# Attention scores as 64x64 matmuls on the four quarters of the tensor array, and the product with v in one group

## The chip, the cores and the metric

The kernel runs on one core of one Trainium2 chip. Its time is the device time of one execution in microseconds (us); the figure for a kernel is the median of its runs. TensorE is written PE in the profile, its weight loads PEld, VectorE DVE, ScalarE ACT, GpSimd POOL, and SP is the engine whose queue issues nearly all transfers.

## What is computed

A sliding-window attention (4 sequences of 576 tokens, 8 heads of 64, each token sees itself and the 63 tokens before it), then a gated product, then a soft mixture of experts.

```python
scores = scale * np.matmul(q, k.transpose(0, 1, 3, 2))
mask = (rel >= 0) & (rel < 64)                      # rel = query position - key position
attn = softmax(np.where(mask, scores, -1e9))
x = np.matmul(attn, v)                              # [4, 8, 576, 64] -> x [2304, 512]
x = ((x @ w_a) * (x @ w_b)) @ w_out                 # w_a, w_b [512, 1536], w_out [1536, 512]
logits = x @ phi                                    # 8 experts x 4 slots
slots = softmax(logits, axis=0).T @ x               # through each expert: relu(slots @ w1) @ w2
out = softmax(logits, axis=1) @ expert_outputs      # [2304, 512]
```

## The kernel before, in words

The 2304 tokens are 18 tiles of 128. A tile has two blocks of 64 tokens (`b` = 0, 1). A block's window is the 128 keys of the block before it and of itself. The 8 heads are four pairs (`u` = 0 to 3); the two heads of a pair (`h` = 0, 1) lie in the two halves of the partitions, 64 rows each.

**Scores** (`att_q`, `att_k`, `att_s`). `att_q` and `att_k` transpose q and k of a tile, so that a head's 64 features lie on partitions. `att_s` makes for each block and pair the scores [2 heads x 64 queries, 128 keys] in a PSUM bank for each block, `s0` and `s1`. The first six tiles (`t < NPLAIN`) do this with two matmuls of 64 rows and 64 columns each (line 279): head 0 on the array's upper left quarter, head 1 on its lower right one. The twelve tiles from 6 on do it with one matmul of the full 128x128 array (line 283); for these, `att_q` writes q between zeros (`att_z` clears the place once), so that the other head's features add nothing. A 32-bit matmul shows in the trace as two records. Then DVE adds the mask and takes the row maximum (line 294), ACT takes the exponential (line 301), `att_n` divides, `att_pt` transposes the probabilities (`tp`), and `att_pv` multiplies them with v (line 342) into the bank `xps`: 8 matmuls of 128 rows and 64 columns for block 0 as soon as its probabilities are transposed, and 8 for block 1 one slot of the schedule later. The two heads write the two column halves in turn.

**The rest.** `glu` is the gated product: for a tile 3 blocks of 512 columns for w_a and for w_b, each 12 matmuls (`psa`, `psb`, line 449). The `r_` functions turn its result (`tg`), make logits (`lps`, line 485, 32 columns of the array for each of four matmuls side by side) and keep running sums (`ups`). Last come the experts, whose weights (`xw`) are fetched into places that the attention and the gated product leave.

**What sets the order.** The start is written out by hand in the text `STARTUP`, for all five engines: `As0` is the next piece of `att_s` of tile 0, `Av0.1` that of `att_pv` of tile 0, block 1; `Sa2.0` issues the load of a piece of w_a, `Da2.0` decodes it, `Po3` is a piece of the work on w_out. It covers attention of tiles 0 to 4 and the decoding of the gated product's weights. From there on only PE's order is fixed, by the numbered slots of `at(...)`; a scheduler orders the other engines. A tile's scores stand at slot `s`, its products with v at `s + 3` and `s + 4`, and its gated product begins at `s + 6` or later. SP issues transfers in the order of its queue; the two places for v (`lda` for the window of block 0, `ldb` for that of block 1) are single, so that the next tile's v waits until `att_pv` has read this tile's.

Of the kernel before, what the change touches and what calls it, by code (L numbers as in the profile page):

```python
# [20 lines left out]
P = 128  # L21
STOP = 0
STARTUP = """
    Ak0 Tq0 Aq0 Tq0 Sb0.0 Aq0 Sa0.2 Db0.0 Ak0 Sb0.2 Db0.0 Ak0 As0 Da0.2 As0 Da0.2 Tq1 Db0.0 Db0.2 Db0.0
    Tq1 Sa0.0 Sa0.1 Aq1 As0 As0 Tq2 Db0.0 As0 Db0.0 Ak1 Da0.2 Db0.0 An0.0 An0.0 Ak1 Aq1 Ak1 As0 Da0.2
    Db0.2 Db0.2 As1 Db0.2 Da0.0 Db0.2 An0.1 As1 Ak2 Da0.2 Da0.0 An0.0 As1 Da0.0 Tq2 Db0.2 Da0.2 Da0.1
    Sb0.1 Aq2 As1 Da0.2 An0.1 Ap0.0 Da0.0 Da0.0 Sb0.3 Aq2 Tv0 Db0.1 Ak2 An0.1 Ap0.0 Da0.1 Db0.2 Ap0.1
    Db0.3 Da0.0 An1.0 An1.0 Ak2 Db0.1 Db0.1 Da0.1 As1 Tv0 Av0.0 Ap0.1 Av0.1 As1 Db0.1 Tq3 As2 Da0.1
    Av0.1 Db0.1 As2 Da0.1 An1.1 An1.1 Db0.1 Ak3 Av0.1 Db0.3 Sa0.3 Da0.1 As2 Da0.0 An1.0 Aq3 Da0.3 Tq3
    Sa1.0 Gb0.0 Sa1.1 Da0.3 Ap1.0 An1.1 Da0.3 Tv1 Tv1 Aq3 Da0.1 Ga0.0 Db0.3 As2 Da0.3 Ap1.0 Ak3 Db0.3  # L30
    Ga0.0 Tq4 Ak3 Sb1.0 Ga0.0 Db0.1 Da0.3 Ap1.1 Da1.0 Da1.1 As3 An2.0 As2 Db0.3 Da1.1 Da1.1 As3 Da0.3
    Db0.3 Gb0.0 Da1.0 Av1.0 Ap1.1 Sa1.2 Av1.1 Sa1.3 Da0.3 As2 Da1.0 Av1.1 Gb0.0 Da1.1 An2.0 Db0.3 Da1.0
    An2.1 Da1.0 Ga0.0 Ga0.0 An2.1 Gb0.0 Da1.1 An2.0 Av1.1 Gb0.0 Tq4 Ap2.0 As3 Db1.0 Da1.0 Ga1.0 Aq4
    Gb1.0 Ak4 Po1 Da1.2 Db1.0 Ga1.0 Ga1.0 Da1.0 Ap2.0 Gb1.0 Db1.0 Da1.1 Tv2 Da1.3 Gb1.0 Da1.2 Ak4 As3
    Sb1.1 Tv2 Db1.0 Da1.1 Aq4 Da1.2 An2.1 Ak4 Ga1.0 Sb1.2 Da1.3 Da1.2 Db1.0 Da1.3 Sb1.3 Ga1.0 Da1.2 As3
    Gb1.0 Da1.2 Da1.3 Ap2.1 Po1 An3.0 Po1 Da1.2 Da1.3 Db1.0 Ga0.1 Db1.0 Po1 Ap2.1 As4 Ga0.1 Po4 Po1
    Ga0.1 As4 Po1 Gb1.0 Da1.3 Av2.0 Db1.1 As3 As4 Da1.3 Db1.2 Po1 An3.0 Db1.1 Db1.1 An3.0 Db1.2 Ga0.1
    Tv3 Ga0.1 Db1.1 Po1 Po3 Db1.3 Db1.2 Po1 Db1.1 Db1.1 Ph0 Db1.3 Db1.2 Av2.1 Gb0.1 Sa2.0 Sa2.1 Ga1.1
    Av2.1 Po4 Ga1.1 Db1.2 Po4 Av2.1 An3.1 Po4 Db1.3 Ga1.1 An3.1 Db1.3 Ga1.1 Db1.1 Ga1.1 Ap3.0 Db1.2 Tv3
    Gb0.1 Ga2.0 Ga2.0 Ga2.0 As4 Db1.2 Po3 Ga2.0 As4 Da2.0 Ga2.0 Po1 An3.1 Db1.3 Po3 Sa2.2 Po4 Ap3.1  # L40
    An4.0 Db1.3 As4 Db1.3 Da2.0 Gb0.1 Ga2.1 Po3 An4.0 Po7 Po4 Po3 Ga2.1 Po3 Po4 Ga2.1 Po3 Gb0.1 Gb0.1
    Ap3.0 Po4 Av3.0 Ga2.1 Da2.1 Da2.1 Ap3.1 Da2.1 Av3.1 Gb2.0 Po3 Gb2.0 Da2.0 Po1 Tv4 Av3.1 Da2.1 Sa2.3
    Gb2.0 Gb2.0 Ri0 Tq5 Po1 Sb2.1 Ga2.1 Av3.1 Da2.0 Ga3.0 Da2.1 Da2.0 Po0 Ga3.0 Da2.2 Gb2.0 Da2.0 Da2.2
    An4.0 Po4 Po3 Gb1.1 Po1 Da2.0 Da2.2 Sb2.0 Gb1.1 Tv4 Da2.1 Gb1.1 Ga3.0 Po5 Da2.3 Da2.2 Po7 Ga3.0
    Da2.2 Po7 Da2.3 Gb1.1 Po7 Da2.2 Po4 An4.1 Tq5 Da2.1 Da2.2 Ga3.0 Po7 Da2.3 An4.1 Ga0.2 Gb1.1 Po0
    Da2.3 Po7 Ap4.0 Ga0.2 Ga0.2 Gb2.1 Po4 Ga0.2 Da2.3 Db2.0 Da2.3 Po4 Sb2.2 Db2.0 Po7 Da2.3 Po0 Ap4.0
    Po5 Ga0.2 Gb2.1 An4.1 Po4 Gb2.1 Gb2.1 Ga0.2 Ga0.2 Db2.0 Po0 Ga0.2 Po3 Po7 Po0 Av4.0 Db2.0 Po0 Ga0.2
    Po6 Ga1.2 Po5 Db2.0 Po5 Ga1.2 Ga1.2 Po3 Ga1.2 Po3 Po5 Po7 Po5 Ga1.2 Po0 Db2.2 Gb2.1 Ga1.2 Po2 Db2.0
    Po5 Db2.2 Po0 Po5 Po3 Ga1.2 Db2.1 Db2.1 Db2.2 Po7 Po7 Gb3.0 Ga1.2 Db2.0 Ga1.2 Db2.1 Gb3.0 Po2 Po7
    Db2.2 Gb3.0 Po0 Db2.1 Ga3.1 Db2.2 Po5 Gb3.0 Po6 Ga3.1 Sb2.3 Po7 Po2 Gb3.0 Po5 Po5 Ga3.1 Db2.1 Po2  # L50
    Po6 Db2.2 Db2.1 Po2 Po2 Po6 Ga3.1 Ap4.1 Ga3.1 Db2.2 Po6 Po6 Po2 Db2.3 Gb3.1 Ga2.2 Ga2.2 Po5 Gb3.1
    Gb3.1 Po5 Po8 Po0 Db2.1 Ak5 Gb3.1 Ga2.2 Db2.3 Po9 Db2.3 Po0 Db2.3 Po0 Ak5 Ga2.2 Ga2.2 Po6 Po0 Gb3.1
    Ap4.1 Po8 Ga2.2 Po2 Gb0.2 Ak5 Gb0.2 Ga2.2 Db2.3 Av4.1 Po8 Po8 Po8 Po2 Gb0.2 Po2 Ga2.2 Po8 Db2.3
    Gb0.2 Po11 Db2.3 Gb0.2 Po2 Gb0.2 Po6 Tv5 Po2 Gb0.2 Po10 Gb0.2 Ga2.2 Tv5 Po2 Po8 Ga3.2 Po9 Gb0.2 Po6
    Ga3.2 Ga3.2 Po6 Po11 Gb1.2 Gb1.2 Po6 Ga3.2 Po9 Po8 Gb1.2 Gb1.2 Ga3.2 Gb1.2 Ga3.2 Po6 Po11 Po9 Po8
    Po10 Po10 Gb1.2 Po9 Po6 Gb1.2 Ga3.2 Po8 Gb1.2 Rt0.0 Po9 Po8 Gb1.2 Ga3.2 Po9 Po9 Gb3.2 Rt0.0 Aq5 Po9
    Po8 Po11 Po10 Av4.1 Po11 Po8 Po11 Gb3.2 Gb3.2 Gb3.2 Aq5 Po11 Gb3.2 Po10 Po9 Ga3.2 Po11 Po9 Po10 Po10
    Gb3.2 Po11 Po10 Po9 Rt0.2 Gb3.2 Po9 Po10 Gb3.2 Rt0.2 Rt0.1 Gb3.2 Rt1.0 Po10 Po10 Gb2.2 Gb2.2 Po10
    Gb2.2 Gb2.2 Gb2.2 Po10 Po11 Gb2.2 Gb2.2 Po11 Gb2.2 Gb2.2 Rt1.0 Po11 Rt0.1 Av4.1 Po11
# [955 lines left out]
```

## Time and profile before

| | us |
|---|---|
| median of 3 runs | 579.15 (578.6 to 579.62) |
| the profiled execution, by its span (no other time of it is listed) | 577.4 |
| PE busy | 540.5 (94%) |
| DVE busy | 297.6 (52%) |
| ACT busy | 229.8 (40%) |
| POOL busy | 76.5 (13%) |

The span runs from the first to the last instruction. The median lies 1.75 us above it, for what lies around the span and for the spread of the runs. Matmuls overlap, so PE's busy time says that PE had work, not that it worked at its peak.

### The profile page before, as it was taken

What the parts mean: (1) busy time and instruction counts of PE and PEld (TensorE: products, weight loads), DVE (VectorE), ACT (ScalarE), POOL (GpSimd) and SP (SyncE); (2) the same over time, 40 slices, a digit from 0 to 9 for tenths busy, and PEclk for the clock granted to TensorE, in tenths of its full rate; (3) what the DMA queues carried; (4) which work ended last, traced back from release to release, by engine and by line L of the source; (5) the groups of instructions that cost most, each with busy time, mean ns of one, the idle gap of its engine ahead of it and who ended that gap; (6) DMA issues with size and microseconds to landing.
All of it is one profiled execution on the core that took longest, in us unless ns stands there. A gap on an engine that the chain in (4) does not pass through costs nothing.

```text
span 577.4 us, 11537 instructions
## 1 busy us (share of the span) xinstructions
PE 540.5 (94%) x4531; PEld 429.9 (74%) x4531; DVE 297.6 (52%) x861; ACT 229.8 (40%) x675; POOL 76.5 (13%) x110
## 2 busy tenths in 40 slices
PE   4588899999999999999999999999999999989993
PEld 3476667889887879787888888888888767953442
DVE  3999999974444444353634443454555311142222
ACT  5767664544524343443523333433454211133013
POOL 4555465331000000000000000000000000020000
PEclk9789899999999999999999999999999999999997
DMA  9975747495030302020212203022212499889997
GB/s 267 266 224 182 242 137 212 145 257 183 0 75 1 75 18 58 18 57 19 56 27 48 56 19 74 17 59 56 56 38 74 152 351 339 317 289 346 341 357 245
DMA packets 110822, 83.00 MB, mean 144 GB/s; under 512 B 77616, under 2 KB 98608, under 8 KB 110768
## 3 DMA queue, kind: packets, MB, share of 16 engines
q1 hardware_dynamic: 109808, 79.12, 46.2%
q0 software_dynamic: 960, 3.15, 1.4%
q8 instruction: 36, 0.59, 0.4%
q14 instruction: 18, 0.15, 0.1%
HBM read 74.38 MB, written 7.86 MB: 142 GB/s over the span
## 4 chain that ended last, share of the span: by engine, by line
PE 77%; DVE 13%; DMA 4%; issue 2%; ACT 1%; SPq 1%; POOL 0%; POOLq 0%; ACTq 0%
PE psb L449 24%; PE psa L449 23%; PE tg L142 5%; PE s L283 4%; PE xps L342 3%; PE lps L485 3%; PE tp L142 2%; PE ups L560 2%; PE h L883 2%; DVE w L374 2%; DVE w L378 2%; PE ops L917 2%; DMA st<-in_moe_w_a_dram 2%; DVE w L368 1%; PE tq L142 1%
## 5 line engine op out<-in xcount | busy, mean ns | idle before, releaser
L449 PE MATMUL psa<-wha,x 128*128 128x512 f32 (+1 forms) x576 | 160.4, 347 | 2.1 <-DVE x L352 1.2
L449 PE MATMUL psb<-whb,x 128*128 128x512 f32 (+1 forms) x576 | 161.3, 348 | 1.1 <-DVE g L459 1.1
L449 PEld LDWEIGHTS psa<-wha,x 128*128 128x128 f32 x576 | 101.4, 189 | 18.3 <-DVE x L352 2.0
L449 PEld LDWEIGHTS psb<-whb,x 128*128 128x128 f32 x576 | 101.3, 190 | 14.7 <-issue 2.4
L449 PE MATMUL psa<-wla,x 128*128 128x512 f32 (+1 forms) x288 | 97.3, 338 | 1.2 <-POOL wla L424 1.2
L449 PE MATMUL psb<-wlb,x 128*128 128x512 f32 (+1 forms) x288 | 97.2, 337 | 0.0
L459 DVE TENSOR_TENSOR g<-psb,asb 128x512 f32<-128x512 f32 (+1 forms) x57 | 37.7, 661 | 89.2 <-PE psb L449 75.0
L455 ACT COPY asb<-psa 128x512 f32<-128x512 f32 (+1 forms) x57 | 32.1, 563 | 103.8 <-PE psa L449 103.4
L301 ACT ACTIVATE pr<-pr,nmx 128x128 f32<-128x128 f32 x144 | 55.9, 391 | 36.7 <-DVE nmx L294 36.7
L449 PEld LDWEIGHTS psa<-wla,x 128*128 128x128 f32 x288 | 54.7, 190 | 6.9 <-POOL wla L424 2.1
L449 PEld LDWEIGHTS psb<-wlb,x 128*128 128x128 f32 x288 | 54.8, 190 | 4.6 <-POOL wlb L424 0.2
L471 ACT COPY gT<-tg 128x512 f32<-128x512 f32 x54 | 31.4, 584 | 37.1 <-PE tg L142 37.0
L252 POOL COPY kTs<-kTs 128x256 f32<-128x256 f32 x17 | 8.2, 480 | 270.8 <-DVE kTs L263 266.1
L142 PE MATMUL tg<-ident,g 128*128 128x128 f32 x216 | 33.9, 280 | 0.7 <-DVE g L459 0.4
L331 DVE COPY pT<-tp 128x512 f32<-128x512 f32 x13 | 9.0, 691 | 47.9 <-PE tp L142 47.9
L294 DVE CUSTOM_DVE_ANT_0 pr<-s,masks 128x128 f32<-128x128 f32 x144 | 32.6, 285 | 1.8 <-PE s L283 1.0
L142 PEld LDWEIGHTS tg<-ident,g 128*128 128x128 f32 x216 | 24.7, 146 | 10.5 <-issue 7.3
L301 ACT ACTIVATION_READ_ACCUMULATOR pr<-pr,nmx 128x1 f32 x144 | 27.2, 189 | 0.0
L329 ACT COPY pT<-tp 128x512 f32<-128x512 f32 x23 | 13.4, 583 | 29.7 <-PE tp L142 29.7
L142 PE MATMUL tp<-ident,pr 128*128 128x128 f32 x144 | 22.9, 282 | 1.1 <-POOL pr L319 1.1
L283 PE MATMUL s<-kTs,qTs 128*128 128x128 f32 x192 | 23.5, 275 | 0.0
L350 ACT CAST x<-xps 128x512 fp32r<-128x512 f32 x18 | 10.5, 584 | 30.8 <-PE xps L342 30.8
(138 smaller groups left out, 754.3 us busy)
## 6 DMA issues: line engine op xcount, KB each, us to landing
xw<-in_moe_w_dram SPq DMA_DIRECT2D x39, 512.0 KB, 6.8
xw<-in_moe_w_dram SPq DMA_DIRECT2D x50, 256.0 KB, 5.9
st<-in_moe_w_b_dram SPq DMA_DIRECT2D x12, 512.0 KB, 5.3
st<-in_moe_w_a_dram SPq DMA_DIRECT2D x12, 512.0 KB, 5.9
st<-in_moe_w_out_dram SPq DMA_DIRECT2D x12, 512.0 KB, 4.7
out_dram<-ob SPq DMA_DIRECT2D x18, 256.0 KB, 3.9
ldq<-in_q_dram SPq DMA_DIRECT2D x16, 256.0 KB, 3.6
ldk<-in_k_dram SPq DMA_DIRECT2D x16, 256.0 KB, 3.4
```

The costliest lines, as they stand in the source:

```text
L142: nc.tensor.transpose(o, i, ident)
L283: nc.tensor.matmul(sp[:, u], lhsT=qT[:, 2 * u + b].rearrange("p h w -> p (h w)"), rhs=kTs[:, t % 2, u, W * b:W * b + P],)
L294: nc.vector.tensor_tensor_reduce(out=pr[:, u], in0=sps[b][:, u], in1=mk, scale=1.0, scalar=HUGE, op0=ALU.add, op1=ALU.min, accum_out=nmx[: ...
L301: nc.scalar.activation(out=pr[:, u], in_=pr[:, u], func=ACTF.Exp, scale=-1.0, bias=nmx[:, i:i + 1], accum_out=sm[:, i:i + 1],)
L329: nc.scalar.copy(out=pT, in_=tp)
L342: nc.tensor.matmul(xps[W * h:W * h + W, u, W * b:W * b + W], lhsT=vt[:, 2 * u + h, :], rhs=st["pT", b][:, u, W * h:W * h + W],)
L374: nc.vector.scalar_tensor_tensor(out=i, in0=hi, scalar=-(1 << 30), in1=i, op0=ALU.bitwise_and, op1=ALU.bitwise_or)
L449: nc.tensor.matmul(ps[:, cols], lhsT=l[:, kk], rhs=r, start=(n == 0), stop=(n == 3 * KD - 1))
L455: nc.scalar.copy(out=asb[:, cols], in_=ps[:, cols])
L459: nc.vector.tensor_tensor(out=gts[t][:, gcols], in0=ps[:, cols], in1=pas.pop((t, fg))[:, cols], op=ALU.mult)
L471: nc.scalar.copy(out=gT, in_=tp)
L485: nc.tensor.matmul(lps[32 * i:32 * i + 32], lhsT=wphi[:, 4 * fg + i], rhs=gT[:, i], start=(n == 0), stop=(n == len(fgs) - 1),)
```

## The change

- All 18 tiles take their scores from 64x64 matmuls, four for each pair: rows by head, columns by block. Head `h` has the PSUM bank `s{h}`, and block `b` the partition half; before, a bank was a block's and a partition half a head's. For the first six tiles this replaces the two-quarter form, for the other twelve the full one.
- `att_s` is cut after pairs 1 and 3, where it was cut after block 0 and block 1. Each half now writes both banks.
- The mask is stored as four blocks of 64 keys, two of which are picked for a tile, and DVE reads and writes the 128 keys of a row as two runs of 64.
- `att_q` is one ACT copy for every tile, into two buffers in turn; DVE's half of the copy and `att_z` are gone.
- `att_pv` is one group of 16 matmuls at the place where block 1's 8 stood. The transposed probabilities (`pT`) get a third buffer, since both are held until then.

```diff
-            nc.gpsimd.affine_select(
-                out=m, in_=m, pattern=[[0, 2], [1, P]], compare_op=ALU.is_gt,
...
+        qT = qTs[:, t % 2]
+        nc.scalar.activation(out=qT, in_=tq, func=ACTF.Copy, scale=-SCALE)
         sts[t] = {"qT": qT}
-        for h in range(2):
-            r = slice(W * h, W * h + W)
-            src = tq[r].rearrange("p u (b w) -> p (u b) w", b=2)
-            if h:
-                nc.vector.tensor_scalar(out=qT[r, :, h], in0=src, scalar1=-SCALE, scalar2=None, op0=ALU.mult)
-            else:
-                nc.scalar.activation(out=qT[r, :, h], in_=src, func=ACTF.Copy, scale=-SCALE)
...
-        for b in range(2):
-            sp = ps_s.tile([P, 4, P], F32, tag=f"s{b}", name=f"s{b}")
-            sps.append(sp)
-            for u in range(4):
-                if t < NPLAIN:
-                    for h in range(2):
-                        r = slice(W * h, W * h + W)
-                        nc.tensor.matmul(
-                            sp[r, u], lhsT=qT[r, u, W * b:W * b + W], rhs=kTs[r, t % 2, u, W * b:W * b + P],
-                        )
-                    continue
-                nc.tensor.matmul(
-                    sp[:, u], lhsT=qT[:, 2 * u + b].rearrange("p h w -> p (h w)"),
-                    rhs=kTs[:, t % 2, u, W * b:W * b + P],
-                )
-            yield
+        sps = [ps_s.tile([P, 4, P], F32, tag=f"s{h}", name=f"s{h}") for h in range(2)]
+        for u in range(4):
+            for h in range(2):
+                r = slice(W * h, W * h + W)
+                for b in range(2):
+                    c = slice(W * b, W * b + W)
+                    nc.tensor.matmul(
+                        sps[h][c, u], lhsT=qT[r, u, c], rhs=kTs[r, t % 2, u, W * b:W * b + P],
+                    )
+            if u % 2:
+                yield
...
-    def att_pv(t, b):
+    def att_pv(t):
...
+        for b in range(2):
+            vt = loaded[t]["b" if b else "a"]
+            c = slice(W * b, W * b + W)
+            for u in range(4):
+                for h in range(2):
+                    nc.tensor.matmul(
+                        xps[W * h:W * h + W, u, c], lhsT=vt[:, 2 * u + h, :], rhs=st["pT", h][:, u, c],
+                    )
...
-        at(s + 3, att_pv, t, 0)
         at(s + 3, att_pt, t, 1)
-        at(s + 4, att_pv, t, 1)
-        if t == NPLAIN:
-            at(s - 3, att_z)
+        at(s + 4, att_pv, t)
...
-    Db0.3 Da0.0 An1.0 An1.0 Ak2 Db0.1 Db0.1 Da0.1 As1 Tv0 Av0.0 Ap0.1 Av0.1 As1 Db0.1 Tq3 As2 Da0.1
+    Db0.1 Db0.1 Da0.1 As1 Tv0 Ap0.1 Av0 As1 Db0.1 Tq3 As2 Da0.1 Av0 Db0.1 As2 Da0.1 An1.1 An1.1 Db0.1 Ak3 Av0
```

The order of the instructions shows it at three places. On PE, the scores of tile 7 stand between the gated product (`psb`) and the logits (`lps`), before:

```order
L449 MATMUL psb<-wlb_1321,x 128x256
L449 MATMUL psb<-whb_1320,x 128x256
L283 MATMUL s_2384<-kTs,qTs 128x128 x4
L283 MATMUL s_2389<-kTs,qTs 128x128 x4
L485 MATMUL lps<-gT,wphi 32x128 x12
L449 MATMUL psa<-wha_324,x 128x512
```

and in the changed kernel (the last four of eight such rows, two matmuls each, for the two blocks):

```order
L259 MATMUL s_2390<-kTs,qTs 64x128 x2
L259 MATMUL s_2391<-kTs,qTs 64x128 x2
L259 MATMUL s_2390<-kTs,qTs 64x128 x2
L259 MATMUL s_2391<-kTs,qTs 64x128 x2
L460 MATMUL lps<-gT,wphi 32x128 x12
L424 MATMUL psa<-wha_325,x 128x512
```

Eight matmuls of the whole array have become sixteen of a quarter, at the same place. On PE again, the product with v of a later tile, block 0 (`lda`), before:

```order
L449 MATMUL psa<-wla_674,x 128x512
L449 MATMUL psa<-wha_673,x 128x512
L342 MATMUL xps<-pT,lda 64x64 x8
L142 MATMUL tp<-ident,pr 128x128 x4
L560 MATMUL ups<-g,dt 32x384 x4
```

and in the changed kernel, where that place has no `xps` any more and the 8 matmuls stand a slot later, ahead of block 1's:

```order
L424 MATMUL psb<-wlb_838,x 128x512
L424 MATMUL psb<-whb_837,x 128x512
L320 MATMUL xps<-pT,lda 64x64 x8
L320 MATMUL xps<-pT,ldb 64x64 x8
L139 MATMUL tq<-ident,ldq 128x128 x4
```

In the start, on PE, the scores of tile 4 (`s_702`, `s_720`) and the product with v of tile 2, before:

```order
L279 MATMUL s_720<-kTs,qTs 64x128 x8
L342 MATMUL xps<-pT,lda 64x64 x8
L449 MATMUL psa<-wha_673,x 128x512
L449 MATMUL psa<-wla_674,x 128x512
L449 MATMUL psa<-wha_673,x 128x512
L142 MATMUL two<-ident,wo 128x128 x4
L342 MATMUL xps<-pT,ldb 64x64 x8
```

and in the changed kernel:

```order
L259 MATMUL s_703<-kTs,qTs 64x128 x2
L259 MATMUL s_704<-kTs,qTs 64x128 x2
L424 MATMUL psa<-wha_674,x 128x512
L424 MATMUL psa<-wla_675,x 128x512
L424 MATMUL psa<-wha_674,x 128x512
L139 MATMUL two<-ident,wo 128x128 x4
L320 MATMUL xps<-pT,lda 64x64 x8
L320 MATMUL xps<-pT,ldb 64x64 x8
```

The reading of `lda` has moved behind three matmuls of the gated product and four transposes. SP's queue and the other engines keep their order, but for the operations that are gone or new and three swaps of neighbours.

## Rows read from the trace of the kernel before

**Rows 1.** Windows: length; busy PE, PEld, DVE, ACT, POOL; clock, DMA share, GB/s.
```profile
14.00:112.00 98.00, 82.51 (x628) 63.94 (x629) 96.93 (x208) 61.12 (x165) 51.60 (x49) 0.93 0.71 205
112.00:455.00 343.00, 342.10 (x2930) 288.75 (x2929) 163.97 (x542) 135.45 (x430) 14.38 (x23) 1.00 0.23 58
455.00:577.00 122.00, 109.45 (x928) 71.79 (x926) 31.55 (x92) 25.80 (x66) 4.75 (x15) 0.98 0.94 324
```

**Rows 2.** PE's timeline, full-array scores of two tiles: start, length, line, operation, records.
```profile
200.44 1.95 PE L283 MATMUL s<-kTs,qTs 128*128 128x128 f32 x16
202.31 0.86 PE L485 MATMUL lps<-gT,wphi 128*32 128x128 f32 x24
...
227.86 1.95 PE L283 MATMUL s<-kTs,qTs 128*128 128x128 f32 x16
229.64 0.27 PE L142 MATMUL dps<-ident,e 128*128 128x128 f32 x1
```

**Rows 3.** PE's timeline, two-quarter scores of tiles 4 and 5, and their neighbours.
```profile
57.70 0.40 PE L449 MATMUL psa<-wha,x 128*128 128x512 f32 x1
58.02 1.09 PE L279 MATMUL s<-kTs,qTs 64*64 64x128 f32 x16
59.05 0.69 PE L342 MATMUL xps<-pT,lda 128*64 128x64 f32 x16
...
145.00 1.96 PE L279 MATMUL s<-kTs,qTs 64*64 64x128 f32 x32
```

**Rows 4.** PE's timeline around a product with v, and transposes behind a gated product.
```profile
209.58 0.60 PE L142 MATMUL tp<-ident,pr 128*128 128x128 f32 x4
...
212.87 0.39 PE L449 MATMUL psa<-wla,x 128*128 128x512 f32 x1
213.09 0.39 PE L449 MATMUL psa<-wha,x 128*128 128x512 f32 x1
213.41 0.69 PE L342 MATMUL xps<-pT,lda 128*64 128x64 f32 x16
214.03 0.66 PE L142 MATMUL tp<-ident,pr 128*128 128x128 f32 x4
```

**Rows 5.** Tiles s, lps, xps: one record's ns (min/median/max), first and last start.
```profile
L279 PE MATMUL s<-kTs,qTs x192: 269/269/473, 8.5 to 146.7; 64*64 64x128 f32 x192
...
L485 PE MATMUL lps<-gT,wphi x432: 272/273/298, 146.9 to 511.3; 128*32 128x128 f32 x144
...
L342 PE MATMUL xps<-pT,lda x288: 222/222/366, 24.6 to 449.5; 128*64 128x64 f32 x144
```

**Rows 6.** Tiles qTs, kTs and tp: copies on ACT, DVE and POOL.
```profile
L243 DVE TENSOR_SCALAR qTs<-tq x12: 694/695/697, 165.9 to 426.6; 64x512 f32<-64x512 f32 x12
L234 ACT ACTIVATE qTs<-tq x6: 577/588/632, 5.2 to 135.4; 128x512 f32<-128x512 f32 x6
L223 POOL MEMSET qTs<- x1: 952/952/952, 147.1 to 147.1; 128x1024 f32 x1
...
L263 DVE COPY kTs<-tk x13: 678/691/692, 119.7 to 430.4; 128x512 f32<-128x512 f32 x13
...
L331 DVE COPY pT<-tp x13: 690/691/692, 159.3 to 450.4; 128x512 f32<-128x512 f32 x13
```

**Rows 7.** Timelines of SP and ACT, and pieces of the chain that ended last.
```profile
59.77 0.38 SPq L207 DMA_DIRECT2D lda<-in_v_dram  x1
...
61.36 0.95 SPq L408 DMA_DIRECT2D st<-in_moe_w_a_dram  x2
65.05 0.37 SPq L207 DMA_DIRECT2D ldb<-in_v_dram  x1
...
61.36 4.23 DMA st<-in_moe_w_a_dram
...
72.90 0.65 ACT L366 ACTIVATE w<-st 128x512 f32<-128x512 f32 x1
...
111.21 0.43 PE pp L591 x8
```

More of the change, by code (lines that the diff above doesn't have):

```diff
@@ L125, in swa_glu_softmoe_kernel @@
     ri = const.tile([P, P], F32, name="ri")
-    masks = const.tile([P, 2, P], F32, name="masks")
+    masks = const.tile([P, 4, W], F32, name="masks")
     sel = const.tile([P, 2, 4, NS], F32, name="sel")
@@ L153, in build_ident @@
             nc.gpsimd.affine_select(
-                out=m, in_=m, pattern=[[0, 2], [1, P]], compare_op=ALU.is_gt,
+                out=m[:, 3], in_=m[:, 3], pattern=[[-1, W]], compare_op=ALU.is_ge,
+                fill=BIG, base=0, channel_multiplier=1,
+            )
+            nc.gpsimd.affine_select(
+                out=m[:, 0:3], in_=m[:, 0:3], pattern=[[0, 3], [1, W]], compare_op=ALU.is_gt,
                 fill=BIG, base=0, channel_multiplier=-1,
             )
-            nc.gpsimd.affine_select(
-                out=m, in_=m, pattern=[[0, 2], [-1, P]], compare_op=ALU.is_ge,
-                fill=BIG, base=W, channel_multiplier=1,
-            )
-        nc.gpsimd.memset(masks[:, 1, 0:W], BIG)
+            nc.gpsimd.memset(m[:, 1 - h], BIG)
     def build_ri():
@@ L215, in swa_glu_softmoe_kernel @@
     xts = {}
-    qTs = att.tile([P, 2 * 4 * P], F32, name="qTs", bufs=1)
+    qTs = att.tile([P, 2, 4, P], F32, name="qTs", bufs=1)
     kTs = att.tile([P, 2, 4, W + P], F32, name="kTs", bufs=1)
-    NPLAIN = NFIRST + 2
-    def att_z():
-        nc.gpsimd.memset(qTs, 0.0)
     def att_q(t):
@@ L299, in att_s @@
             for u in range(4):
-                i = 4 * b + u
+                i = 4 * h + u
                 nc.scalar.activation(
@@ L305, in att_s, with att_n @@
             yield
-    def att_n(t, b):
+    def att_n(t, hh):
         st = sts[t]
-        h = slice(4 * b, 4 * b + 4)
+        h = slice(4 * hh, 4 * hh + 4)
         rs = small.tile([P, 4, 1], F32, tag="rs", name="rs")
@@ L324, in att_pt @@
         for u in range(4):
-            transpose(tp[:, u], st["pr"][b][:, u])
+            transpose(tp[:, u], st["pr"][hh][:, u])
         yield
-        pT = att.tile([P, 4, P], F32, tag="pT", name="pT")
-        if b == 0 or t <= NFIRST:
+        pT = att.tile([P, 4, P], F32, tag="pT", name="pT", bufs=3)
+        if hh == 0 or t <= NFIRST:
             nc.scalar.copy(out=pT, in_=tp)
@@ L331, in att_pt @@
             nc.vector.tensor_copy(pT, tp)
-        st["pT", b] = pT
-    def att_pv(t, b):
+        st["pT", hh] = pT
+    def att_pv(t):
         st = sts[t]
-        if b == 0:
-            st["x"] = ps_t.tile([P, 4, P], F32, tag="x", name="xps", bufs=1)
-        xps = st["x"]
-        vt = loaded[t]["b" if b else "a"]
-        for u in range(4):
-            for h in range(2):
-                nc.tensor.matmul(
-                    xps[W * h:W * h + W, u, W * b:W * b + W],
-                    lhsT=vt[:, 2 * u + h, :],
-                    rhs=st["pT", b][:, u, W * h:W * h + W],
-                )
-        if b == 1:
-            yield
-            x = xp.tile([P, 2, 4, P], F32R, tag="x", name="x")
-            nc.scalar.copy(out=x[:, 0], in_=xps)
-            yield
-            nc.vector.tensor_tensor(out=x[:, 1], in0=xps, in1=x[:, 0].bitcast(F32), op=ALU.subtract)
-            xts[t] = (x[:, 0], x[:, 1])
-            del sts[t], loaded[t]
+        xps = ps_t.tile([P, 4, P], F32, tag="x", name="xps", bufs=1)
+        for b in range(2):
+            vt = loaded[t]["b" if b else "a"]
+            c = slice(W * b, W * b + W)
+            for u in range(4):
+                for h in range(2):
+                    nc.tensor.matmul(
+                        xps[W * h:W * h + W, u, c], lhsT=vt[:, 2 * u + h, :], rhs=st["pT", h][:, u, c],
+                    )
+        yield
+        x = xp.tile([P, 2, 4, P], F32R, tag="x", name="x")
+        nc.scalar.copy(out=x[:, 0], in_=xps)
+        yield
+        nc.vector.tensor_tensor(out=x[:, 1], in0=xps, in1=x[:, 0].bitcast(F32), op=ALU.subtract)
+        xts[t] = (x[:, 0], x[:, 1])
+        del sts[t], loaded[t]
     whi, wlo = {}, {}
@@ L585, in project_phi @@
         yield
-        wT = att.tile([P, 4, P], F32, tag="pT", name="wT")
+        wT = att.tile([P, 4, P], F32, tag="pT", name="wT", bufs=3)
         nc.scalar.copy(out=wT, in_=tp)
```

88 lines of the change are left out of this document (39 added, 49 removed).

## Prediction

> **What bounds the kernel now.** I read the windows of the trace first, cut where the stages change [rows 1]. From 14 to 112 us DVE is busy for 96.93 of 98 us: the start, in which the weights are decoded, is DVE's. From 112 to 455 us PE is busy for 342.10 of 343 us at the full clock, DVE for 164 and ACT for 135: here a microsecond less on PE is a microsecond less in all, as long as PE finds no new wait. All work of the attention for tiles 5 to 17 lies in this stretch. After 455 us the DMA engines are busy to 94%: the experts' weights go into places that the attention and the gated product have left. Nothing is changed there; it starts when the attention ends, so I take it to move as a whole.
>
> Then the timelines of PE. A tile's scores on the full array are 16 records in 1.95 us; the last lasts 0.27 us, so they start 0.112 us apart. From the first to the next work it is 1.78 us where full-array work follows, 1.87 where the 32-column logits follow [rows 2]. The two-quarter form of the first tiles shows 16 records in 1.09 us and 32 in 1.96 [rows 3]: 0.87 us for 16 more, or 8 pairs 0.109 us apart. Two quarters overlap fully, but each works on half the rows and half the columns, so that form is no faster than the full one. The logits show four column groups at once: 24 records in 0.86 us, one lasting 0.272 [rows 2, 5], so 0.59 us from first to last, six sets of four about 0.118 apart. The product with v shows two column groups that share all rows, with different moving data: 16 records in 0.69 us, one lasting 0.222 [rows 4, 5], so 0.47 us for 8 pairs, 0.059 each. Every change of the array's shape costs something: from the gated product into the product with v it is 0.32 us from start to start, where 0.22 is the normal step, and four transposes behind it take 0.66 us instead of 0.60 [rows 4]; the two-quarter scores show the same 0.32 [rows 3]. So 0.10 to go in and 0.06 behind.
>
> **The change part by part.**
>
> *Scores, tiles 6 to 17.* 8 full matmuls (16 records) become 16 quarter matmuls (32 records), four quarters in turn. No row shows all four. I take sets of four at the pace of the two-quarter pairs, since the logits run four deep at about that pace. 32 records are then 8 sets, and the block lasts as long as the 16-record block of 8 pairs, 58.02 to 59.05, 1.03 us [rows 3]. With 0.10 in and 0.06 out it is 1.19 us instead of 1.78: 0.59 less. This holds for ten tiles (the order of the instructions shows transposes, the running sums or the gated product behind them). Behind the scores of two tiles the logits stand, which change the array's shape in either kernel: 1.13 instead of 1.87, 0.74 less. Sum: 5.9 + 1.5 = 7.4 us. The bounds: at a set every 0.118 us, the logits' step, 0.07 us less per tile, 0.9 in all; if no more than two quarters overlap, a loss (below).
>
> *Scores, tile 5.* 16 pairs become 8 sets: 0.87 us [rows 3].
>
> *Scores, tiles 0 to 4.* In DVE's stretch: PE gets done earlier and waits longer. I take 0. If the start followed PE, five times 0.87 would be the bound, 4.4 us.
>
> *Product with v, tiles 5 to 17.* A group costs 0.10 + 0.62 (213.41 to 214.03) + 0.06 = 0.78 us. Two groups become one whose second 16 records cost 0.47: 0.31 less, 13 times, 4.0 us. Tile 4's first group lay in DVE's stretch and now joins the second, at about 121 us, when PE is the bound: the chain goes over to PE's work at 111.21 [rows 7]. That gives 0.5 back.
>
> *What comes later.* Block 0's product now waits a slot longer, and nothing but block 1's stood between it and the copy of `xps`, so the gated product gets its x as before. Both heads' scores are complete only at the end of the block, but the block is shorter by as much.
>
> *Other engines.* DVE loses twelve copies of 0.695 us and POOL one clearing of 0.95 us; ACT keeps one copy for each tile, 0.588 us for the whole [rows 6]. All three are covered: DVE is busy for less than half of PE's stretch [rows 1]. Uncovered, DVE's twelve would be 8.3 us more gain. The mask's and scores' rows are read as two runs of 64: DVE's copy of kTs in four runs takes 691 ns as does its copy of one run [rows 6], so 0.
>
> *SP's queue.* The load of the next v into `lda` waits for the product that read it. In the start that product of tile 2 moves behind three matmuls and four transposes, to where `ldb` is read now. SP issues `lda` at 59.77 now and `ldb` at 65.05 [rows 7], so `lda` goes from 59.77 to about 65.0, and what is queued behind it moves by 5.2 us: a piece of w_out, phi and two pieces of w_a. The first w_a goes out at 61.36, takes 4.23 us and is decoded by ACT at 72.90 [rows 7]: 7.3 us of slack, of which 2.1 stay. I take 0; without that slack it would be 5.2.
>
> Sum: 7.4 + 0.9 + 4.0 - 0.5 = 11.8 us. The profiled execution has a span of 577.4, which would be 565.6. The median, 579.15, lies 1.75 above the span; I let that stand: 567.4 us.
>
> The Trainium skill bears on the step that no row shows. "TensorE: Matmul & The Clock Gate", section "Why this matters for your kernels", says that row and column tiling compose, with 10.6 times measured for 16 tiles of 32x32; by that four quarters overlap as I assume, and no run here shows it yet.
>
> **The rivals.**
>
> *Only two of the four overlap.* Either the two row halves that feed one column half take turns, or the weight loads set the pace: each record has its own load of 64 columns, twice as many as now. For it: the pairs seen are diagonal, or share rows, never a column half with different rows. Against: the logits issue four loads in a set. The block is then that of 32 records, 1.03 + 0.87 = 1.90 us, and with 0.10 and 0.06 it is 2.06: ten times +0.28, twice 2.00 against 1.87, tile 5 nothing: +3.1 us. With v's -4.0 and +0.5 that leaves 578.7 us.
>
> By "TensorE: Matmul & The Clock Gate", section "LDWEIGHTS", a load takes its number of columns over 1.2 GHz, 53 ns for 64 columns, which is this rival by loads alone. The trace disagrees: the product with v starts a pair of records, each with a load of 64 columns, every 0.059 us [rows 4], 29 ns a load.
>
> *The quarters run one after another* (slower). The place is the same block: 32 records 0.109 us apart are 3.5 us, with 0.16 for the ends 3.65, and 0.16 to go in and out: 3.81 against 1.78 ten times, 3.75 against 1.87 twice, 3.65 against 1.90 for tile 5: +25.8 us, and 3.5 back from v: 601 us. It decides from a block that is 0.27 us longer than now (3.5 us over 13 tiles), which is hardly above the pace of two at once. Against it: two overlap in every two-quarter row.
>
> *The start gets longer.* The queue's 5.2 us use up the slack, since DVE has no idle time to catch up in [rows 1]; or the first half of the scores, which writes both banks, waits in the start for DVE to read the second bank. For it: `lda` is on the chain that ended last now. At 3 us, the 5.2 less about 2 of slack: 570.4; at worst 572.6.
>
> **How the numbers follow.** Four overlap and the start holds: 0.76, around 567.4. The start longer: 0.11, 568 to 572.6. Two overlap: 0.09, 578.7. One after another: 0.04, 601. The range reaches down by part of the 4.4 us that the start could give, to 564, and up into the longer start, to 571.5; it leaves out the two rivals without four at once and the tail of the longer start, under 0.2. A measurement of this kernel tells 0.2% (1.2 us) from no change. Faster: 0.87 from the first two cases, and a little of the third case, whose 578.7 is within the bound: faster 0.88, same 0.07, slower 0.05.
>
> **What would show it.** In the profile after: a tile's scores as 32 records in about 1.1 us at lines of `att_s`, in sets of four (right), in 1.96 (two overlap) or in 3.7 (none). One `xps` group of 32 records, 1.15 to 1.2 us, for each tile. PE's stretch without new waits, DVE's end of the start still at 111 to 112 us, the first w_a piece decoded near 72.9, the experts' weights starting about 12 us earlier. I am wrong if the sets are wider apart than 0.12 us, if PE waits for the mask or for v after 112 us, or if the chain passes through SP's queue at 65 us.

## The result, and the profile after

| | before | after |
|---|---|---|
| median of 4 runs each, us | 579.21 (578.6 to 579.62) | 566.39 (565.3 to 567.37) |
| the profiled execution, span, us | 577.4 | 564.7 |
| PE busy, us | 540.5 | 525.3 |
| DVE busy, us | 297.6 | 287.6 |

After over before is 0.978, with a 95% interval of 0.9765 to 0.9796: 12.8 us less, and by the interval 11.8 to 13.6. The forecast was 567.4 in 564.0 to 571.5.

The windows of the changed kernel, cut where its stages change (length; busy PE, PEld, DVE, ACT, POOL; clock, DMA share, GB/s), answer to [rows 1]:

```profile
14.00:111.00 97.00, 78.48 (x606) 60.49 (x608) 95.91 (x206) 60.73 (x161) 51.25 (x49) 0.93 0.71 205
111.00:442.00 331.00, 330.10 (x3140) 277.17 (x3144) 153.96 (x530) 134.81 (x430) 13.43 (x22) 1.00 0.26 60
442.00:564.00 122.00, 110.31 (x941) 72.39 (x933) 32.19 (x92) 25.98 (x67) 4.76 (x15) 0.98 0.95 323
```

The start is DVE's as before (95.91 of 97 us) and the end the transfers'. The stretch between them is PE's as before (330.10 of 331, granted clock 1.00), and it is the one that got shorter; the first load of an expert's weights from `in_moe_w_dram` goes out at 443.1 us where it was 455.1. PE gained no wait that counts. PE's waits from 112 to 515 us, the longest first (waiting line, releaser, us in total, times, longest), name DVE's running sums and `uT`, and neither the mask nor v:

```profile
PE ups L535 <- DVE dt L527: 0.8, 2, 0.6
PE tu L139 <- DVE uT L820: 0.8, 2, 0.4
PE lps L460 <- DVE acc L545: 0.7, 1, 0.7
```

PE's timeline (start, length, line, operation, records) shows the scores of a tile followed by the logits, those of one followed by transposes, and a product with v between gated product and transposes. They answer to [rows 2], [rows 3] and [rows 4]:

```profile
188.57 0.39 PE L424 MATMUL psb<-whb,x 128*128 128x512 f32 x1
188.89 0.69 PE L320 MATMUL xps<-pT,lda 128*64 128x64 f32 x16
189.40 0.64 PE L320 MATMUL xps<-pT,ldb 128*64 128x64 f32 x16
189.97 0.66 PE L139 MATMUL tq<-ident,ldq 128*128 128x128 f32 x4
...
198.65 1.10 PE L259 MATMUL s<-kTs,qTs 64*64 64x128 f32 x32
199.69 0.86 PE L460 MATMUL lps<-gT,wphi 128*32 128x128 f32 x24
...
225.01 1.10 PE L259 MATMUL s<-kTs,qTs 64*64 64x128 f32 x32
226.04 0.33 PE L139 MATMUL dps<-ident,e 128*128 128x128 f32 x1
226.21 0.60 PE L139 MATMUL tg<-ident,g 128*128 128x128 f32 x4
```

A tile's scores are 32 records where 16 stood, in 1.10 us where it was 1.95, and the product with v is 32 records from 188.89 to 189.97, 1.08 us. One score record still lasts 269 ns, so the last starts 0.83 us after the first. None of the three signs that the prediction named as proof against it shows: from the second set on the sets are 0.109 us apart (below), PE waits for neither the mask nor v, and the chain that ended last goes over PE between 61.81 and 69.15 us, not through SP's queue. The queue in the start, answering to [rows 7], in SP's and ACT's timelines:

```profile
64.97 0.38 SPq L205 DMA_DIRECT2D lda<-in_v_dram  x1
...
66.56 0.95 SPq L383 DMA_DIRECT2D st<-in_moe_w_a_dram  x2
...
72.53 0.66 ACT L341 ACTIVATE w<-st 128x512 f32<-128x512 f32 x1
```

### The profile page after: what moved, and what is told of

It is laid out like the page before. It is cut to its first block, busy times and chain, and to the rows that moved or that the text cites. A ratio compares the mean times of both kernels' runs of the same rounds, so it can differ in the third digit from the quotient of the medians.

```text
span 564.7 us, 11892 instructions
## 1 busy us (share of the span) xinstructions
PE 525.3 (93%) x4723; PEld 414.8 (73%) x4723; DVE 287.6 (51%) x849; ACT 229.3 (41%) x675; POOL 75.3 (13%) x110
## 4 chain that ended last, share of the span: by engine, by line
PE 74%; DVE 15%; DMA 5%; issue 2%; ACT 1%; SPq 0%; POOL 0%; POOLq 0%; ACTq 0%
PE psb L424 24%; PE psa L424 23%; PE tg L139 5%; DMA xw<-in_moe_w_dram 3%; PE xps L320 3%; PE lps L460 3%; PE ups L535 2%; PE s L259 2%; PE h L855 2%; DVE w L349 2%; DVE w L353 2%; PE tp L139 2%; DVE w L343 2%; DVE pr L272 1%; DVE w L345 1%
## 5 line engine op out<-in xcount | busy, mean ns | idle before, releaser
L259 PE MATMUL s<-kTs,qTs 64*64 64x128 f32 x576 | 23.7, 301 | 5.5 <-DVE nmx L272 3.1
L272 DVE CUSTOM_DVE_ANT_0 pr<-s,masks 128x128 f32<-128x128 f32 x112 | 24.9, 285 | 2.6 <-PE s L259 2.6
L259 PEld LDWEIGHTS s<-kTs,qTs 64*64 64x64 f32 x576 | 18.2, 147 | 9.4 <-issue 4.2
```

The source lines that it names most:

```text
L259: nc.tensor.matmul(sps[h][c, u], lhsT=qT[r, u, c], rhs=kTs[r, t % 2, u, W * b:W * b + P],)
L272: nc.vector.tensor_tensor_reduce(out=pr[:, u].rearrange("p (a k) -> p a k", a=2), in0=sps[h][:, u].rearrange("p (a k) -> p a k", a=2), in1 ...
```

## The experiments

Each kernel computes everything that the reference asks for. The time of a whole run moves by 1 us and more, but one stretch can be read to a few hundredths. It runs from the first record of tile 5's scores to the last matmul of the gated product, both from PE's timeline, and holds all attention that the forecast priced except that of tiles 0 to 4. In the two kernels of the case its ends are, in the changed one and then in the one before:

```profile
145.19 1.10 PE L259 MATMUL s<-kTs,qTs 64*64 64x128 f32 x32
...
496.44 0.29 PE L424 MATMUL psb<-whb,x 128*128 128x256 f32 x1
```

```profile
508.65 0.29 PE L449 MATMUL psb<-whb,x 128*128 128x256 f32 x1
```

with 145.00 of [rows 3] as the beginning before. All kernels (times in us; the interval is that of the ratio to the kernel before, which was run again beside each group of kernels, with medians from 579.2 to 579.6):

| kernel | median | ratio, interval | stretch from, to | length |
|---|---|---|---|---|
| before | 579.21 | | 145.00, 508.65 | 363.65 |
| changed | 566.39 | 0.978, 0.9765 to 0.9796 | 145.19, 496.44 | 351.25 |
| before_pv | 575.69 | 0.9927, 0.9902 to 0.9952 | 146.35, 506.18 | 359.83 |
| pv_apart | 570.51 | 0.9836, 0.9817 to 0.9855 | 146.43, 500.77 | 354.34 |
| pairs_diag | 573.12 | 0.9888, 0.9872 to 0.9905 | 146.09, 503.69 | 357.60 |
| pairs_rows | 573.52 | 0.9895, 0.988 to 0.9911 | 146.14, 503.72 | 357.58 |
| pairs_cols | 573.2 | 0.9882, 0.986 to 0.9905 | 147.03, 504.64 | 357.61 |
| one_by_one | 586.03 | 1.0115, 1.0093 to 1.0136 | 144.77, 515.03 | 370.26 |
| runs_of_two | 568.11 | 0.9811, 0.9791 to 0.9832 | 147.74, 499.90 | 352.16 |
| start_pairs | 567.83 | 0.98, 0.9774 to 0.9825 | 146.41, 497.67 | 351.26 |
| start_one | 568.07 | 0.9807, 0.9789 to 0.9825 | 146.77, 498.04 | 351.27 |
| queue_free | 566.94 | 0.9781, 0.9765 to 0.9797 | 146.05, 497.34 | 351.29 |
| copy_split | 566.34 | 0.9783, 0.9766 to 0.98 | 145.69, 496.96 | 351.27 |
| pv_next | 565.28 | 0.9763, 0.9746 to 0.9781 | 146.81, 496.65 | 349.84 |

Where a kernel changes no work on PE in the stretch (start_pairs, start_one, queue_free, copy_split), its length agrees to 0.04 us. The start does not: nine kernels have the changed kernel's start unaltered (changed, pv_apart, the three with pairs, one_by_one, runs_of_two, copy_split, pv_next), and in their profiles tile 5's scores begin anywhere from 144.77 to 147.74. What the median of such a kernel has beyond the length of its stretch lies closer together: 215.07 to 216.17 in these nine, and 215.56 in the kernel before.

### The two halves of the change

**before_pv** is the kernel before with v in one group.

```diff
-        at(s + 3, att_pv, t, 0)
...
+        at(s + 4, att_pv, t, 0)
         at(s + 4, att_pv, t, 1)
...
-        pT = att.tile([P, 4, P], F32, tag="pT", name="pT")
+        pT = att.tile([P, 4, P], F32, tag="pT", name="pT", bufs=3)
...
```

> The kernel before with one part of the change: for tiles 5 to 17 the product with v stands in one group of 32 records, a slot later, with a third pT buffer; scores, q copies and tiles 0 to 4 as before. By my step, 0.31 us for each of 13 tiles: 4.0 us less, 575.2. Rival: the later place of block 0's product makes the gated product wait for x, and nothing is gained, 579.2.

**pv_apart** is the changed kernel with v in two groups.

```diff
-        at(s + 4, att_pv, t)
+        at(s + 4, att_pv, t, (0,))
+        at(s + 5, att_pv, t, (1,))
...
```

> The changed kernel with the product with v of tiles 5 to 17 in two groups again, one slot apart; scores as quarters. By my step, 0.31 us more for each of 13 tiles: 4.0 us above the changed kernel, 570.4, and so 8.8 below the one before, which is what the scores alone bring. Rival: the merging brought nothing and the scores all, then 566.4.

Both came out: 575.69 for 575.2, 570.51 for 570.4. In the stretch, merging alone takes 3.82 us off (363.65 to 359.83), where 4.0 was expected, and the scores on top of it 8.58 (359.83 to 351.25), where 8.3 was (tiles 5 to 17). Taking the groups apart again, a slot later than the kernel before had them, adds 3.09, less than 4.0: from tile 9's product to tile 10's it is 0.28 more (270.68 to 297.08 against 268.30 to 294.42), but the last four tiles, whose work stands in another order, add only some 0.5 together; why is not shown. PE does not wait for x in before_pv: its timeline has the merged group at the pace of the changed kernel.

```profile
191.22 0.39 PE L449 MATMUL psb<-whb,x 128*128 128x512 f32 x1
191.54 0.69 PE L342 MATMUL xps<-pT,lda 128*64 128x64 f32 x16
192.05 0.64 PE L342 MATMUL xps<-pT,ldb 128*64 128x64 f32 x16
192.62 0.66 PE L142 MATMUL tq<-ident,ldq 128*128 128x128 f32 x4
```

### Is it four quarters at once?

Four kernels differ from the changed one in nothing but the order of the 16 score matmuls of tiles 5 to 17. All have this loop in place of the three loops over `u`, `h` and `b`:

```diff
+        for n, (u, h, b) in enumerate(order):
+            r, c = slice(W * h, W * h + W), slice(W * b, W * b + W)
+            nc.tensor.matmul(
+                sps[h][c, u], lhsT=qT[r, u, c], rhs=kTs[r, t % 2, u, W * b:W * b + P],
+            )
+            if n % 8 == 7:
+                yield
```

The orders, first **pairs_diag**:

```diff
+        order = [(u, h, h ^ d) for d in range(2) for u in range(4) for h in range(2)] if t > NFIRST else [(u, h, b) for u in range(4) for h in range(2) for b in range(2)]
```

> The changed kernel with the 16 score matmuls of tiles 5 to 17 in another order: only the two diagonal quarters in turn, then only the two others. Every matmul, mask and copy is the same. If the gain is that four quarters run at once, no more than two do here: 16 pairs 0.109 us apart, 1.70 us from the first record to the last where it is 0.84, 0.86 more for each of 13 tiles, 11.2 in all: 577.6. Rival: the smaller matmuls gain by themselves, in whatever order: 566.4.

**pairs_rows**:

```diff
+        order = [(u, h, b) for h in range(2) for u in range(4) for b in range(2)] if t > NFIRST else [(u, h, b) for u in range(4) for h in range(2) for b in range(2)]
```

> As the run with diagonal pairs, but each pair shares a row half (one head, both column halves). If any two different quarters overlap, the block is again 1.70 us from first to last: 577.6. Rival: quarters that share rows take turns, 3.4 us, up to 599.

**pairs_cols**:

```diff
+        order = [(u, h, b) for b in range(2) for u in range(4) for h in range(2)] if t > NFIRST else [(u, h, b) for u in range(4) for h in range(2) for b in range(2)]
```

> As the run with diagonal pairs, but each pair shares a column half (both heads, one query block, two banks). No row of the kernel before showed such a pair. If any two different quarters overlap: 1.70 us from first to last, 577.6. Rival, the one named in the prediction: the two row halves that feed one column half take turns, 3.4 us, up to 599.

**one_by_one**:

```diff
+        order = [(u, h, b) for h in range(2) for b in range(2) for u in range(4)] if t > NFIRST else [(u, h, b) for u in range(4) for h in range(2) for b in range(2)]
```

> The changed kernel with the score matmuls of tiles 5 to 17 ordered so that all four of one quarter come before the next quarter's. By the theory that only different quarters overlap, 32 records 0.109 us apart: 3.4 us from first to last for 0.84, less the few that overlap where the quarter changes (three places of 0.08): 2.3 to 2.5 more for each of 13 tiles, 30 to 33 us: 596 to 599. Rival: a record waits only for its own load and for room in the queue, so that matmuls of one quarter also run behind each other faster than 0.109: below 590.

The same block in pairs_diag and in one_by_one, by PE's timeline:

```profile
200.54 1.59 PE L257 MATMUL s<-kTs,qTs 64*64 64x128 f32 x32
202.06 0.86 PE L458 MATMUL lps<-gT,wphi 128*32 128x128 f32 x24
```

```profile
201.19 2.56 PE L257 MATMUL s<-kTs,qTs 64*64 64x128 f32 x32
203.68 0.86 PE L458 MATMUL lps<-gT,wphi 128*32 128x128 f32 x24
```

The order alone moves the time by 6.7 to 7.1 us (pairs) and by 19.6 (one by one), so the smaller matmuls do not gain by themselves: the gain needs different quarters in turn. The three kinds of pair cost the same (357.58 to 357.61), so quarters that share rows, quarters that share columns and quarters that share neither overlap alike. The rival that two row halves feeding one column half take turns falls.

My price was wrong, though, and these four expectations were missed: 573.1 to 573.5 for 577.6, and 586.0 for 596 to 599. 1.70 us from first to last record was expected with pairs and 3.4 one by one, and 1.32 (1.59 less 0.27) and 2.29 (2.56 less 0.27) were measured. The rival in one_by_one had the number (below 590) but not the reason: records of one quarter stay 0.109 us apart. The start times of the records, from the trace (ns after the block's first):

```
changed     0 7 14 20 | 160 167 174 180 | 270 276 283 290 | 379 ... | 815 822 829 835
pairs_diag  0 7 | 160 167 | 270 276 | 379 385 | 488 495 | 500 507 | 597 604 | 660 667 | 706 713 | 770 776 | 815 822 | 879 885 | 988 995 | ... | 1315 1322
one_by_one  0 160 269 378 487 493 596 653 706 762 815 871 981 986 1090 1146 1199 1256 1308 1365 1474 1480 1583 ... 2076 2185 2295
```

In one_by_one a quarter has 8 records. At 493, right behind the fifth, a new sequence of steps of 0.160 and then 0.109 begins between the old one's last three (596, 706, 815): the next quarter runs while three records of this one still wait. The same happens at 500 with pairs, where three records of each of two quarters wait. And in one_by_one the record with the first bank's signal, the program's 16th, is the 19th to start: records start out of the program's order when their quarter is free. That three records of a quarter can wait without holding up the others is read into these starts; this I had not thought of, and it gave a theory to test.

**runs_of_two** sends two matmuls (four records) of a quarter before the next quarter's.

```diff
+        order = [(u + v, h, b) for u in (0, 2) for h in range(2) for b in range(2) for v in range(2)] if t > NFIRST else [(u, h, b) for u in range(4) for h in range(2) for b in range(2)]
```

> The changed kernel with the score matmuls of tiles 5 to 17 in runs of two matmuls (four records) of one quarter, the four quarters in turn. In the runs with pairs and with one quarter at a time the next quarter's first record started right behind the fifth record of the one before, so three records of a quarter waited and did not hold up other quarters. If that room is for each quarter, four records of each pass at once and the block stays near 0.89 us: 566.4 to 567.2. Rival: the room is three records in all, then blocks of 1.60 us, 0.77 more for each of 13 tiles: 576.4.

```profile
201.38 1.17 PE L257 MATMUL s<-kTs,qTs 64*64 64x128 f32 x32
202.48 0.86 PE L458 MATMUL lps<-gT,wphi 128*32 128x128 f32 x24
```

1.17 less 0.27 is 0.90 us from first to last, for 0.89 expected and 1.60 by the rival; the stretch is 0.91 us longer than the changed kernel's, 13 times 0.07. So there is room for three waiting records for each quarter, not three in all. The median, 568.11, is above the 566.4 to 567.2 that I had expected, and 1.7 us above the changed kernel's. Of that 0.9 is in the stretch; the rest is within the spread of what lies outside it (215.95, for 215.07 to 216.17 in the nine kernels).

### What was priced at nothing

**start_pairs** and **start_one** have the same loop, with the orders of pairs_diag and one_by_one for tiles 0 to 4 alone.

```diff
+        order = [(u, h, b) for u in range(4) for h in range(2) for b in range(2)] if t > NFIRST else [(u, h, h ^ d) for d in range(2) for u in range(4) for h in range(2)]
```

> The changed kernel with the score matmuls of tiles 0 to 4 alone in diagonal pairs: 0.86 us more of TensorE for each, 4.3 in all, in the start. By my step the start is VectorE's and nothing changes: 566.4 within 0.4. Rival: the start follows TensorE, up to 570.7.

```diff
+        order = [(u, h, b) for u in range(4) for h in range(2) for b in range(2)] if t > NFIRST else [(u, h, b) for h in range(2) for b in range(2) for u in range(4)]
```

> The changed kernel with the score matmuls of tiles 0 to 4 alone ordered one quarter after another. In the run with that order in tiles 5 to 17 a block lasted 2.30 us from first to last record for 0.84: 1.46 us more TensorE work for each of five tiles, 7.3 in all, three times what the run with pairs put into the start. If the start is VectorE's: 566.4, within the 1 us by which the start of tile 5's scores moved between profiles of kernels with the same start (144.8 to 147.0 us). Rival: the start follows TensorE in part; if the 1.4 us that the median rose with pairs was real, three times as much, 570 to 571; all of it, 573.7.

By the blocks as they turned out, start_pairs adds 0.49 us to each of five blocks, 2.4 in all (not the 4.3 that I had expected of it), and start_one 1.46, 7.3 in all. The window of the start, in start_one and then in the changed kernel:

```profile
14.00:112.00 98.00, 88.30 (x604) 71.34 (x603) 96.46 (x205) 61.56 (x163) 52.73 (x49) 0.97 0.70 204
```

```profile
14.00:112.00 98.00, 79.48 (x613) 61.19 (x612) 96.91 (x209) 61.28 (x163) 51.25 (x49) 0.93 0.71 204
```

PE has 8.8 us more in it, and DVE's busy time is 0.45 us less. The medians rose by 1.4 and by 1.7 us, so both expectations were missed (566.4 within 0.4; 566.4 or 570 to 571), with intervals that overlap the changed kernel's. Outside the stretch the two have 216.57 and 216.80 us, above all nine kernels with the start unaltered. Three times the work made hardly more of it. That nothing of it reaches the end was too sharp: some 1 us does, if anything, which is near the uncertainty, and not the 7.3. The granted clock of the window was 0.97 with start_one for 0.93, so part of PE's work there may have run faster than in the changed kernel; how much that hides is not shown.

**queue_free** has the load of tile 3's v into `lda` issued behind phi and the first two pieces of w_a. Of the two lines of `STARTUP` only the words around the change are shown.

```diff
-Ga0.1 Tv3 Ga0.1
+Ga0.1 Ga0.1
...
-Sa2.0 Sa2.1 Ga1.1
+Sa2.0 Sa2.1 Tv3 Ga1.1
```

> The changed kernel with the load of tile 3's v into lda issued behind phi and the two pieces of w_a instead of ahead of them, so that they go out some 5 us earlier, near 61 us as in the kernel before; the order on TensorE is the same. By my step the 5.2 us that the queue had lost were covered by slack: 566.4 within 0.4. Rival: the late queue cost part of them, then 561.2 to 566.

SP's timeline, and ACT's first decode of that w_a:

```profile
48.48 1.16 SPq L383 DMA_DIRECT2D st<-in_moe_w_a_dram  x2
65.23 0.37 SPq L205 DMA_DIRECT2D lda<-in_v_dram  x1
```

```profile
73.39 0.66 ACT L341 ACTIVATE w<-st 128x512 f32<-128x512 f32 x1
```

The pieces went out at 48.48, 18 us earlier than in the changed kernel (not at 61 as I had written: `lda` was all that they waited behind). The decode came at 73.39 where it was 72.53, and the ratio is 0.9781 for 0.978. Even with these two pieces 18 us earlier nothing changes, so the 5.2 us that the queue lost cost nothing.

**copy_split** gives DVE half of the q copy of tiles 6 to 17 again.

```diff
-        nc.scalar.activation(out=qT, in_=tq, func=ACTF.Copy, scale=-SCALE)
...
+        if t < NFIRST + 2:
+            nc.scalar.activation(out=qT, in_=tq, func=ACTF.Copy, scale=-SCALE)
+            return
+        nc.vector.tensor_scalar(out=qT[W:P], in0=tq[W:P], scalar1=-SCALE, scalar2=None, op0=ALU.mult)
+        nc.scalar.activation(out=qT[0:W], in_=tq[0:W], func=ACTF.Copy, scale=-SCALE)
```

> The changed kernel with the q copy of tiles 6 to 17 cut by partitions again: 64 by ScalarE, 64 by VectorE, which gets back its twelve copies of 0.695 us, 8.3 us of work. By my step they are covered: 566.4 within 0.4. Rival: VectorE's queue delays something that TensorE waits for, up to 574.7.

The instructions of tile qTs (ns min/median/max, first and last start):

```profile
L229 DVE TENSOR_SCALAR qTs<-tq x12: 694/694/695, 164.7 to 415.5; 64x512 f32<-64x512 f32 x12
```

The twelve copies are back, 8.3 us of DVE's time, and neither the median (566.34) nor the stretch (351.27) moves. They were covered, as the prediction had it.

### A version that goes further

**pv_next** moves the product with v of ten tiles beside work of the same kind: behind the transposes of q and ahead of the logits, or a slot later ahead of the running sums.

```diff
-        at(s + 4, att_pv, t)
+        late = t == 8 or 10 <= t <= 14
+        at(s + 4 + late, att_pv, t)
...
-            at(s + 5, load, t + 1, "ab")
+            at(s + 5 + late, load, t + 1, "ab")
...
+        evs = events[n]
+        pv = [e for e in evs if e[0] is att_pv]
+        if pv and any(e[0] in (r_l, r_u) for e in evs):
+            evs = [e for e in evs if e[0] is not att_pv]
+            i = min(i for i, e in enumerate(evs) if e[0] in (r_l, r_u, load) and e[1][-1:] != ("qk",))
+            evs = evs[:i] + pv + evs[i:]
...
```

> The changed kernel with the product with v of ten tiles moved beside other matmuls that use a part of the columns: behind the transposes of the next q and right ahead of the logits (tiles 5, 7, 9 and 15), or a slot later right ahead of the running sums (tiles 8 and 10 to 14). If the price of a change of the array's shape is paid per change, two changes become one for each: from the trace of the changed kernel 0.318 + 0.153 + 0.165 + 0.203 + 0.007 become 0.231 + 0.109 + 0.2 + 0.152 + 0.007, 0.15 us less for each, 1.5 in all: 564.9. Rival: x comes too late for the gated product and TensorE waits: 566.4 or more.

PE's timeline in pv_next, and below it the two places in the changed kernel that it joins:

```profile
298.74 0.60 PE L139 MATMUL tk<-ident,ldk 128*128 128x128 f32 x4
299.27 0.69 PE L320 MATMUL xps<-pT,lda 128*64 128x64 f32 x16
299.79 0.64 PE L320 MATMUL xps<-pT,ldb 128*64 128x64 f32 x16
300.36 0.85 PE L535 MATMUL ups<-g,dt 128*32 128x384 f32 x8
```

```profile
294.10 0.39 PE L424 MATMUL psb<-whb,x 128*128 128x512 f32 x1
294.42 0.69 PE L320 MATMUL xps<-pT,lda 128*64 128x64 f32 x16
...
295.50 0.66 PE L139 MATMUL tq<-ident,ldq 128*128 128x128 f32 x4
...
298.98 0.60 PE L139 MATMUL tk<-ident,ldk 128*128 128x128 f32 x4
299.51 0.85 PE L535 MATMUL ups<-g,dt 128*32 128x384 f32 x8
```

The stretch is 1.41 us shorter, for 1.5 expected, and PE waits for no x. So a change of the array's shape has a price of its own, and a group set beside another that uses part of the columns saves one. The median, 565.28, is the lowest of all; against the changed kernel 1.1 us is within the two intervals, so that it is faster is shown in the stretch and not by the medians.

## Why the prediction was right, point by point

**What bounds.** Right. Nearly the whole gain lies where PE bounds: the stretch lost 12.40 us of the 12.8.

**Scores.** Right in the mechanism, and to a few hundredths in size. Before the logits the block takes 1.04 us from start to next start and 0.09 more to go in, 1.13, as forecast. Before transposes it is 1.03 with 0.09 in and 0.06 behind, 1.18 for 1.19 forecast. Sets of four start 0.160 us and then every 0.109 us apart, as the pairs of the kernel before do. The 0.118 that I read from the logits as a bound was a mean that took in their longer first step: the trace has their six sets at 0, 134, 243, 352, 461 and 570 ns, so they run at 0.109 too. Tile 5 lost 1.96 less 1.10, 0.86 for 0.87. In the stretch the scores brought 8.58 for 8.3; the blocks do not show where the other 0.3 lies.

**Product with v.** Right: a merged group takes 1.08 us for 0.62 + 0.47, and merging alone gave 3.82 us in the stretch for 4.0. That the sum, 12.40 for 12.3, is nearer than either part is luck: the two (8.58 for 8.3, 3.82 for 4.0) miss in opposite directions. Taken the other way round, by pv_apart, the scores bring 9.31 (363.65 to 354.34) and the merging 3.09. Tile 4's whole group stands in PE's stretch, as the chain had made me expect:

```profile
121.12 0.69 PE L320 MATMUL xps<-pT,lda 128*64 128x64 f32 x16
121.63 0.64 PE L320 MATMUL xps<-pT,ldb 128*64 128x64 f32 x16
122.20 0.39 PE L424 MATMUL psb<-whb,x 128*128 128x256 f32 x1
```

It stood there with 16 records before; 0.5 us was the price of the others.

**SP's queue.** Right in the result, with the slack mis-sized. `lda` went out at 64.97 for 65.0 forecast, the first w_a at 66.56, and its decode began at 72.53 (72.90 before). I had taken 4.23 us for that load from a step of the chain. The time from this one issue to its landing is longer, before and then in the changed kernel:

```profile
DMA to landing us min/median/max: 5.7/5.7/5.7
...
DMA to landing us min/median/max: 5.8/5.8/5.8
```

So the slack was 5.8 us and not 7.3 (61.36 + 5.7 to 72.90), and 0.2 of it were left where I had 2.1 (66.56 + 5.8 to 72.53). That it held so narrowly was luck. That it cost nothing is shown by queue_free: with the load 18 us earlier the decode came no earlier. The step of the chain was no real wait: it has DVE's line 368 wait for this load at 65.59, but the same instruction (line 343 in the changed kernel) ran at 65.25 there, before the load was even issued:

```profile
65.63 0.41 DVE L368 TENSOR_SCALAR w<-w 128x512 f32<-128x512 f32 x1
...
65.25 0.41 DVE L343 TENSOR_SCALAR w<-w 128x512 f32<-128x512 f32 x1
```

So nothing shows `lda` on the way to the end, which the rival of a longer start leaned on.

**Other engines.** Right: copy_split.

**The start.** I took 0 for five blocks on PE. start_one shows that little of added work there reaches the end. Whether less work shortens the start is told by what lies outside the stretch: 215.56 us before and 215.14 in the changed kernel, 0.42 less, within the 1.1 us by which nine kernels with the same start differ. So 0 was the right choice between 0 and 4.4. Whether it is exactly 0 is open: the 12.40 of the stretch less the 0.5 that tile 4's group was to cost, a price that no run shows by itself, make 11.9 where the medians give 12.8, and the 0.9 between them is as large as the ratio's uncertainty.

**The rivals.** The two without four at once fell with the first row of 32 records in 1.10 us. Their prices, 578.7 and 601, assume that quarters named in turn do not overlap, which no order of the program brings about, so no run tests them. My expectations for the runs with other orders used the same sums and were too high (573 for 577.6, 586 for 596 to 599). The step behind that was that a record behind a busy quarter holds up all that follow; three may wait before that happens.

The trace bears out the sentence of the Trainium skill that I leaned on beside the rows ("TensorE: Matmul & The Clock Gate", section "Why this matters for your kernels", that row and column tiling compose): four records in sets 0.109 us apart. The rule of its section "LDWEIGHTS", 53 ns for a load of 64 columns, spoke for a rival only if it is read as a pace, one load after another. As a pace the trace disagrees: the four loads of a set start within 0.02 us of each other, a record of one lasts 0.133 us (median), and a set takes 0.109 us, 27 ns for each load.

## What to carry to other kernels

Where matmuls use a quarter of the array, name four different quarters in turn: then the order of the program, not the number of instructions, makes them overlap. Two matmuls (four records) of one quarter in a row cost 0.07 us a block here, four (eight records) 1.46. Count the changes of the array's shape, and put groups that use part of the columns side by side. Take the landing of a transfer from its own row, not from a step of the chain, whose releasers are inferred. To judge a change of 1 us, measure a stretch between two marks on the bound engine, not the whole run.

## What the runs showed of the hardware that I had not expected

- A quarter that is busy lets three of its records wait while records behind them start on other quarters, as far as these orders tell: with one matmul of each quarter in turn the block takes 0.83 us from the first start to the last, with two 0.90, with two quarters in turn 1.32, with all four matmuls of a quarter in a row 2.29. So these score records, 32-bit on 64x64 quarters, start out of the program's order, the 16th as the 19th in one_by_one. The Trainium skill ("TensorE: Matmul & The Clock Gate", section "The mechanism") says that matmuls start and end strictly in the program's order; the trace disagrees for the starts.
- Quarters that share a column half, with different rows and banks, overlap as well as diagonal ones (357.61 and 357.60 us for the stretch).
- A product with v beside other part-column work costs 0.14 us less (1.41 us over ten tiles).
- The start, written out for five engines, ends anywhere in 3 us (144.77 to 147.74) in one profile each of nine kernels that share it, while the stretch that PE bounds repeats to 0.04 us.
